# Eight of the token-pair loads of a gated linear attention are issued from ScalarE's queue

## The chip, the cores and the metric

The kernel runs on one core of one Trainium2 chip. The metric is the device time of the whole program in microseconds, lower is better; each kernel is timed in several runs and the median is compared. A profile is one further execution, recorded by the hardware profiler; its span runs from the first to the last instruction of the program, and its own device time is a little longer than its span.

A core has five engines that each work through their own list of instructions in order: TensorE (PE; its weight loads are shown as PEld), VectorE (DVE), ScalarE (ACT), GpSimd (POOL) and SyncE (SP). They wait for each other through semaphores. DMAs are issued here by SyncE and by ScalarE, each into a queue of its own, and both queues are carried by the core's 16 DMA engines.

## The reference

A recurrence with a decaying state for 4 batches of 8 heads, 768 tokens and 48 features, and then a mixer on its output:

```python
for t in range(S):
    state = alpha[:, :, t, :, None] * state + np.einsum('bhd,bhe->bhde', k[:, :, t], v[:, :, t])
    y[:, :, t] = np.einsum('bhd,bhde->bhe', q[:, :, t], state)
...
x = y.transpose(0, 2, 1, 3).reshape(B, S, H * D)
u = x + (x.transpose(0, 2, 1) @ U @ V).transpose(0, 2, 1)
out = u + np.maximum(u @ w_ch1, 0.0) @ w_ch2
```

U is 768 x 32, V 32 x 768, w_ch1 384 x 1536 and w_ch2 1536 x 384; inputs and output are float32.

## The kernel before

Tokens are worked in chunks of 128, six to a batch. A chunk of a batch needs four loads of 192 KB: its alpha, k, q and v, each into one of 40 buffers called `io`. Where a load is done depends on the batch: for all six chunks of batch 0 and the first four of batch 1 two chunks share a stretch of 256 tokens, and a load takes two neighbouring tokens of four heads per partition, in runs of 96 floats (`pload`, L322). These 40 are the token-pair loads. The other chunks take one token of eight heads per partition (`load`, L329). Weights come by L295 and U and V by L270 to L272.

For a chunk, ScalarE takes the logarithm of alpha (`lt`, L352 for a pair, L523 otherwise), TensorE sums it over time (L361 to L368, or L530 and L532), and ScalarE takes exponentials of the sums, `ai` and `aa` and the decay `tot` over the chunk (L375 to L377, or L540, L541 and L543). GpSimd or VectorE multiply k by `ai` and q by `aa` (`rkq`, L383 or L551) and cast v (`rv`, L263 or L267). TensorE transposes the two products (L400 or L564), which are copied from PSUM (`kqt`, L263 or L265), and multiplies them into scores (L424 or L592), which VectorE masks (`pm`, L435 or L602). The state `st` (L473 or L626) passes from chunk to chunk, and the output of the chunk is formed on TensorE (L497 and L507, or L654 and L659). When a batch's chunks are done comes the mixer: a low-rank product (L674, L688), the sum `ub` (L689), transposes, and two large products with the weights (L737 with its relu in L747 or L749, then L763 with the sum in L769 and the store in L774).

The order of all that is written out. The kernel first adds some 1,050 operations to a list, each with a function that takes the name of an engine, and then walks a table of three-character entries: two characters are the number of an operation, the third is the engine that it goes to (P, A, D, G or S for SyncE). Each engine's instructions stand in the order in which the table names them. For a load, the third character says whose queue issues it:

```python
lambda e: (nc.scalar if e == "ACT" else nc.sync).dma_start(
```

A second table gives the buffers; it is the same for both kernels. The semaphores are set by the framework. For DMAs there are eight, DMAHW0 to DMAHW7: each DMA reports its landing on one of them, and it is issued only when the DMA before it on the same semaphore has landed. Which DMA gets which of the eight is dealt out by the framework in the order of the program. An engine that has already waited for a landing does not wait for it again. PSUM has eight banks, which the table of buffers deals to the operations; an operation that takes over a bank waits for the last reader of what was in it.

Of the kernel before, what the change touches and what calls it, by code (L numbers as in the profile page):

```python
# [13 lines left out]

CODE = "ABCDEFGHIJKLMNOPQRSTUVWXYZabcdefghijklmnopqrstuvwxyz0123456789+-"
TABLE = """
BISA8ABASA-AQgAA9SDjAA+SDlPBQSCcACePBKSCzABCSBBSC1PCdACfAABSChACgADnABDSCjDC4AC3ABJSCiDETABES++EClPDqGCkPBMSCnDEVPBRSC6G
CmDDsPBLSEYAC2ACrPDuABSSC5GCoPCsDDmABOSC8PEWACpDAFGC7PC0ABHSCtPCvPCqDC+ADCPDpGDKAC9DBFSCuDEXAC-PDDDBYSCwPEZGDADDEPDrPBUS
DMPDBDDtADkGDGPBGSDNACxDEaGDHPDFDDPADOADvPCyDBTSD8AEbPDIDDyPDJDDLGEcPDoADwDDZPD+PEeAEdDAGPEAABNSDzPDxDAHAEfPBPSD0DDQGEhD
BWSEDGGTABVSDaPAJPGqADbDAASDSPDRGD1PD-AGVPDUDEBAAKADcPD2DGsPGXADdDEUGDTPEgDGWABXSD3PECGEiPD4PEFPGuADVDEjPGtAD5PEHDD9GGvA  # L20
DWPGYABZSD7AGaGD6AEEPEkDElPBgSDYDELPEmPEGADePEMPBaSDXDGZGDfPEIPBcSENDDgPEJDADGEnPBbSDhAEPPGcPEpAEKDGbPDiAAQSEOPGUAEQPEoD
AMSGdAGeDGiPGwGERDEqPAOSESAGjDGfPHaAErPGkDGmPGyPGgDEsAGxGAUSHcPGhDASSE1PE7PHfAG0AE5PAWSE2DGnPHBAEzPE6DBdSGrGGpAGzPGoAEvP
E8DAeSG1AEtPHDPE0DAaSARAANGE9PEuDHGABeSE3PAPGE+AEwDG5PBkSG2PE4DHFAAVGAiSG6DExPHeAFXPHEAATGEyDFZPAXGG7DG9PFYDAgSFBPGlGG4D
FfPAfGFCAE-PHHDFgAAYSFJPG3DHdABiSFAAFdPBoSFaAFFPHIGFeDFKAAcSFhPFGAFHPHzABhSFDPFiAAhGBmSAjAH1PAZGFEDFbPBfSG8GH3AHJPH4AHKP
# [804 lines left out]
```

## Time and profile before

| | |
|---|---|
| median of 3 runs | 159.76 us (158.51 to 160.31) |
| profiled execution | 158.96 us, span 157.2 us, granted clock 1.00 |
| PE | 147.3 us busy, 94% of the span |
| DVE | 107.0 us, 68% |
| ACT | 87.2 us, 55% |
| POOL | 64.6 us, 41% |
| SyncE's DMA queue (q1) | 85808 packets, 28.62 MB |
| ScalarE's DMA queue (q10) | 13536 packets, 2.75 MB |

TensorE counts as busy from the start of a matmul to its modelled end, so a busy share of 94% is not 94% of its peak. A row of the chain of waits gives start, length and what; a row of the timeline gives start, length, engine, line, operation, output and inputs, and in brackets the idle time before it and what ended it. "SPq" and "ACTq" are the sequencers of SyncE and ScalarE that issue DMAs. A row of DMA issues gives the number of DMAs, the size of one, and the median time from issue to landing.

### The profile page before, as it was taken

What the parts mean: (1) busy time and instruction counts of PE and PEld (TensorE: products, weight loads), DVE (VectorE), ACT (ScalarE), POOL (GpSimd) and SP (SyncE); (2) the same over time, 40 slices, a digit from 0 to 9 for tenths busy, and PEclk for the clock granted to TensorE, in tenths of its full rate; (3) what the DMA queues carried; (4) which work ended last, traced back from release to release, by engine and by line L of the source; (5) the groups of instructions that cost most, each with busy time, mean ns of one, the idle gap of its engine ahead of it and who ended that gap; (6) DMA issues with size and microseconds to landing.
All of it is one profiled execution on the core that took longest, in us unless ns stands there. A gap on an engine that the chain in (4) does not pass through costs nothing.

```text
span 157.2 us, 4460 instructions
## 1 busy us (share of the span) xinstructions
PE 147.3 (94%) x1708; PEld 97.5 (62%) x1708; DVE 107.0 (68%) x235; ACT 87.2 (55%) x226; POOL 64.6 (41%) x103
## 2 busy tenths in 40 slices
PE   0898998899999999999999999999999999999991
PEld 0567785566666656667667766666667565566561
DVE  6159998883878658986985948775798463435152
ACT  3858877869797636659788473358713102460000
POOL 8069865656868050275289246155412000000000
PEclk9999999999999999999999999999999999999999
DMA  5999889999999999899999899599780056875234
GB/s 124 323 327 320 230 198 253 277 311 278 251 264 293 246 266 219 151 200 238 206 238 169 139 231 135 116 209 217 145 198 23 0 104 160 263 222 135 74 126 174
DMA packets 99364, 31.64 MB, mean 201 GB/s; under 512 B 93040, under 2 KB 99312, under 8 KB 99344
## 3 DMA queue, kind: packets, MB, share of 16 engines
q1 hardware_dynamic: 85808, 28.62, 77.9%
q10 hardware_dynamic: 13536, 2.75, 9.1%
q8 instruction: 13, 0.21, 0.6%
q14 instruction: 7, 0.06, 0.1%
HBM read 23.89 MB, written 4.72 MB: 182 GB/s over the span
## 4 chain that ended last, share of the span: by engine, by line
PE 77%; SPq 14%; DMA 3%; ACT 1%; issue 1%; POOL 1%; DVE 1%; ACTq 0%
PE ps L763 30%; PE ps L737 29%; SPq L322 12%; DMA io<-in_alpha_dram 3%; PE ps L592 2%; PE ps L564 2%; PE ps L688 2%; PE ps L659 2%; PE ps L530 1%; PE ps L654 1%; PE ps L615 1%; PE ps L708 1%; SPq L270 1%; PE ps L674 1%; PE ps L400 1%
## 5 line engine op out<-in xcount | busy, mean ns | idle before, releaser
L763 PE MATMUL ps<-w_sb,h1t 128*128 128x384 bf16 (+2 forms) x300 | 53.2, 320 | 0.0
L737 PE MATMUL ps<-uT,w_sb 128*128 128x384 bf16 x288 | 51.2, 326 | 0.0
L747 ACT ACTIVATE h1t<-ps 128x384 bf16<-128x384 f32 x57 | 25.9, 501 | 20.9 <-PE ps L737 20.9
L763 PEld LDWEIGHTS <-h1t 128*128 128x128 bf16 x300 | 27.2, 97 | 16.1 <-issue 1.0
L737 PEld LDWEIGHTS <-w_sb 128*128 128x128 bf16 x288 | 27.0, 98 | 16.0
L749 DVE TENSOR_SCALAR h1t<-ps 128x384 bf16<-128x384 f32 x39 | 20.8, 554 | 12.5 <-PE ps L737 12.2
L769 DVE TENSOR_TENSOR io<-ub,ps 128x384 f32<-128x384 bf16 (+2 forms) x25 | 13.2, 536 | 11.3 <-PE ps L763 10.6
L602 DVE TENSOR_TENSOR pm<-ps,maskc 128x512 bf16<-128x512 f32 x28 | 17.7, 683 | 1.0 <-PE ps L592 0.8
L551 POOL TENSOR_TENSOR rkq<-io,ai 128x384 bf16<-128x384 f32 x11 | 10.2, 935 | 14.2 <-DMA io<-in_k_dram 6.6
L689 DVE TENSOR_TENSOR ub<-xb,ps 128x384 bf16<-128x384 bf16 x24 | 12.1, 551 | 2.8 <-PE ps L688 2.7
L551 POOL TENSOR_TENSOR rkq<-io,aa 128x384 bf16<-128x384 f32 x12 | 10.9, 912 | 7.1 <-PE ps L763 3.5
L435 DVE TENSOR_TENSOR pm<-ps,maskp 128x512 bf16<-128x512 f32 x20 | 13.1, 684 | 0.3
L263 ACT CAST xb<-ps 128x192 bf16<-128x192 f32 (+1 forms) x24 | 9.1, 402 | 5.9 <-DVE io L769 2.5
L383 POOL TENSOR_TENSOR rkq<-io,aa 128x384 bf16<-128x384 f32 x9 | 8.2, 918 | 9.2 <-ACT aa L376 4.1
L263 ACT COPY kqt<-ps 128x512 bf16<-128x512 bf16 x18 | 10.5, 595 | 1.5 <-PE ps L400 0.7
L626 POOL TENSOR_TENSOR st<-sm,tot 128x384 bf16<-128x384 f32 x6 | 5.0, 828 | 12.7 <-DVE sm L642 10.7
L267 POOL CAST w_sb<-io 128x384 bf16<-128x384 f32 x16 | 8.1, 514 | 4.6 <-DMA io<-in_moe_w_ch_dram 4.4
L541 ACT ACTIVATE aa<-ps 128x384 bf16<-128x384 f32 x14 | 6.9, 504 | 5.1 <-PE ps L532 4.4
L543 ACT ACTIVATE tot<-ps,off 128x4 f32<-128x4 f32 x22 | 5.9, 278 | 6.4 <-PE ps L532 6.4
L267 POOL CAST rv<-io 128x384 bf16<-128x384 f32 x17 | 8.8, 526 | 1.2 <-DMA io<-in_v_dram 1.1
L265 DVE COPY kqt<-ps 128x512 bf16<-128x512 bf16 x18 | 7.4, 418 | 2.9 <-PE ps L564 1.3
L400 PE MATMUL ps<-ident,rkq 128*128 128x128 bf16 x80 | 8.0, 232 | 1.3 <-ACT lt L352 0.6
(109 smaller groups left out, 214.8 us busy)
## 6 DMA issues: line engine op xcount, KB each, us to landing
io<-in_k_dram SPq DMA_DIRECT2D x24, 192.0 KB, 4.1
io<-in_q_dram SPq DMA_DIRECT2D x24, 192.0 KB, 4.4
io<-in_moe_w_ch_dram SPq DMA_DIRECT2D x24, 192.0 KB, 3.9
io<-in_alpha_dram SPq DMA_DIRECT2D x23, 192.0 KB, 4.2
io<-in_v_dram ACTq DMA_DIRECT2D x13, 192.0 KB, 4.2
out_dram<-io SPq DMA_DIRECT2D x13, 192.0 KB, 2.0
io<-in_v_dram SPq DMA_DIRECT2D x11, 192.0 KB, 3.8
out_dram<-io SPq DMA_DIRECT2D x20, 96.0 KB, 2.2
```

The lines of the kernel that those rows point to most:

```text
L263: nc.scalar.copy(dst, src)
L267: nc.gpsimd.tensor_copy(dst, src)
L322: lambda e: (nc.scalar if e == "ACT" else nc.sync).dma_start(t().rearrange("p (h j) d -> p h (j d)", j=2), src[b, hs, sl, :].rearrange("h ...
L435: nc.vector.tensor_tensor(dst, s2, maskp.to_broadcast([C, 2, 2, C]), op=ALU.mult)
L551: eng.tensor_tensor(dst()[:, :, 0:D], a(), x(), op=ALU.mult)
L602: nc.vector.tensor_tensor(pm()[:, :, par, :], s2, maskc.to_broadcast([C, HP, C]), op=ALU.mult)
L689: P.add(f"u {b}.{c}", lambda e, c=c, hb=hb: nc.vector.tensor_tensor(ub()[:, c, :], xb()[:, c, :], hb()[:, 0:DM], op=ALU.add), r=[hb] + xk( ...
L737: nc.tensor.matmul(hb()[:, 0:TW], lhsT=w1_sb[:, ct, jt * 128 : (jt + 1) * 128], rhs=u_half(uT, ct, tt, b in QUEUE_U), start=(ct == 0), sto ...
L747: nc.scalar.activation(dst, hb()[:, 0:TW], AF.Relu)
L749: nc.vector.tensor_scalar_max(dst, hb()[:, 0:TW], 0.0)
L763: nc.tensor.matmul(hb()[:, 0 : hi - lo], lhsT=h1()[:, jt, c * C : (c + 1) * C], rhs=w2_sb[:, jt, lo:hi], start=(jt == 0), stop=(jt == NJ - 1),
L769: P.add(f"out_{hi - lo} {b}.{c}", lambda e, hb=hb, lo=lo, hi=hi: nc.vector.tensor_tensor(flat(ou)[:, lo:hi], ub()[:, c, lo:hi], hb()[:, 0 ...
```

## The change

Of the 40 token-pair loads in the order of the table, numbers 13, 16, 19, 22, 25, 28, 31 and 34 (every third; the twelfth to the thirty-third when counted from zero) get an A in place of the S. They stay at the same place in the table. Four belong to batch 0 (alpha and v of chunk 2, v of chunk 3, k of chunk 4) and four to batch 1 (alpha and k of chunk 0, v of chunk 1, alpha of chunk 3). The first lines of the diff that differ, in pieces:

```diff
-...ABJSCiDETABES++EClPDq...
+...ABJSCiDETABEA++EClPDq...
-CmDDsPBLSEYAC2A...
+CmDDsPBLAEYAC2A...
```

No other entry differs: TensorE, VectorE and GpSimd have the same instructions in the same order, ScalarE has 8 DMAs more and SyncE 8 fewer. But every DMA's semaphore is dealt anew, so waits differ on all engines.

On ScalarE, near the start (`lt` of the first chunks), the order before (-) and now (+), with the semaphores that an instruction waits for in brackets:

```order
 L376 ACTIVATE aa2_180<-ps_212 128x384
 L352 ACTIVATE lt0_76<-io6_139 128x8x48 [waits DMAHW6_49,Activation_49]
+L322 DMA io12_145<-in_alpha_dram 128x4x96 [waits DMAHW4_49]
+L322 DMA io15_148<-in_v_dram 128x4x96
 L377 ACTIVATE tot2_186<-ps_212 128x8 [waits PE_49]
 L375 ACTIVATE ai1_182<-ps_212 128x384
```

Two loads now stand between the logarithm of io6_139 and the L377 behind it. Further on in ScalarE's order:

```order
 L263 CAST rv1_174<-io10_143 128x384 [waits DMAHW3_49]
+L322 DMA io18_151<-in_v_dram 128x4x96 [waits DMAHW2_49]
 L263 COPY kqt2_190<-ps_212 128x512 [waits PE_49]
-L352 ACTIVATE lt1_77<-io12_145 128x8x48 [waits DMAHW5_49]
+L352 ACTIVATE lt1_77<-io12_145 128x8x48 [waits DMAHW4_49]
 L376 ACTIVATE aa0_178<-ps_212 128x384 [waits Activation_49]
+L322 DMA io21_154<-in_alpha_dram 128x4x96 [waits DMAHW5_49]
 L263 COPY kqt1_189<-ps_212 128x512 [waits PE_49]
```

The load into io21_154, which SyncE issued, now stands behind an exponential (L376), and reports on DMAHW5 (it waits for the DMA before it there). On SyncE the order of the same place was, from the load into io15_148 on:

```order
L322 DMA io15_148<-in_v_dram 128x4x96 [waits DMAHW0_49]
L322 DMA io16_149<-in_q_dram 128x4x96 [waits DMAHW1_49]
L322 DMA io17_150<-in_q_dram 128x4x96 [waits DMAHW2_49]
L322 DMA io18_151<-in_v_dram 128x4x96 [waits DMAHW3_49]
L322 DMA io19_152<-in_k_dram 128x4x96 [waits DMAHW4_49]
L322 DMA io20_153<-in_alpha_dram 128x4x96 [waits DMAHW5_49]
L322 DMA io21_154<-in_alpha_dram 128x4x96 [waits DMAHW6_49]
```

and is now:

```order
L322 DMA io16_149<-in_q_dram 128x4x96 [waits DMAHW1_49]
L322 DMA io17_150<-in_q_dram 128x4x96 [waits DMAHW3_49]
L322 DMA io19_152<-in_k_dram 128x4x96 [waits DMAHW4_49]
L322 DMA io20_153<-in_alpha_dram 128x4x96 [waits DMAHW6_49]
L322 DMA io22_155<-in_q_dram 128x4x96 [waits DMAHW7_49]
L322 DMA io23_156<-in_v_dram 128x4x96 [waits DMAHW0_49]
L322 DMA io25_158<-in_v_dram 128x4x96 [waits DMAHW1_49]
L322 DMA io26_159<-in_q_dram 128x4x96 [waits DMAHW3_49]
L270 DMA ue_in_69<-in_moe_U_dram 64x6x32 [waits DMAHW5_49]
```

The three loads into io15_148, io18_151 and io21_154 are gone from it, and those that stay wait for other semaphores: io19_152 for DMAHW4, on which ScalarE's io12_145 reports, io20_153 for DMAHW6 (ScalarE's io15_148), and ue_in for DMAHW5 (ScalarE's io21_154).

On ScalarE near 80 us of the profile of before, where batch 2 is worked beside the mixer of batch 1, the order is the same but for the waits. Before:

```order
L540 ACTIVATE ai2_183<-ps_212 128x384
L329 DMA io26_159<-in_v_dram 128x8x48 [waits DMAHW2_49]
L543 ACTIVATE tot0_184<-ps_212,off_129 128x4 [waits Pool_49]
L263 CAST rv0_173<-io18_151 128x384 [waits DMAHW6_49]
L540 ACTIVATE ai1_182<-ps_212 128x384 [waits Activation_49]
L543 ACTIVATE tot1_185<-ps_212,off_129 128x4
L541 ACTIVATE aa2_180<-ps_212 128x384
```

and now:

```order
L540 ACTIVATE ai2_183<-ps_212 128x384
L329 DMA io26_159<-in_v_dram 128x8x48 [waits DMAHW4_49]
L543 ACTIVATE tot0_184<-ps_212,off_129 128x4 [waits Pool_49]
L263 CAST rv0_173<-io18_151 128x384 [waits DMAHW1_49]
L540 ACTIVATE ai1_182<-ps_212 128x384 [waits Activation_49]
L543 ACTIVATE tot1_185<-ps_212,off_129 128x4
L541 ACTIVATE aa2_180<-ps_212 128x384
```

The v load into io26_159 waited for DMAHW2 and waits for DMAHW4 now. Which DMA reports on DMAHW4 there is to be seen on GpSimd, in the instructions that read what was loaded:

```order
 L626 TENSOR_TENSOR st3_200<-sm1_196,tot2_186 128x384 [waits DVE_49]
-L551 TENSOR_TENSOR rkq2_81<-io20_153,ai1_182 128x8x48 [waits DMAHW5_49,PE_49]
-L267 CAST rv1_174<-io24_157 128x384 [waits DMAHW7_49]
-L551 TENSOR_TENSOR rkq2_81<-io25_158,aa0_178 128x8x48 [waits DMAHW0_49,Activation_49]
+L551 TENSOR_TENSOR rkq2_81<-io20_153,ai1_182 128x8x48 [waits DMAHW4_49,PE_49]
+L267 CAST rv1_174<-io24_157 128x384 [waits DMAHW2_49]
+L551 TENSOR_TENSOR rkq2_81<-io25_158,aa0_178 128x8x48 [waits DMAHW6_49,Activation_49]
```

The k load into io20_153 reported on DMAHW5 and reports on DMAHW4 now; it is the last DMA on DMAHW4 ahead of the one into io26_159.

More of the change, by code (lines that the diff above doesn't have):

```diff
@@ L16 @@
 TABLE = """
[L17 to L21, printed above, removed]
+BISA8ABASA-AQgAA9SDjAA+SDlPBQSCcACePBKSCzABCSBBSC1PCdACfAABSChACgADnABDSCjDC4AC3ABJSCiDETABEA++EClPDqGCkPBMSCnDEVPBRSC6G
+CmDDsPBLAEYAC2ACrPDuABSSC5GCoPCsDDmABOSC8PEWACpDAFGC7PC0ABHACtPCvPCqDC+ADCPDpGDKAC9DBFSCuDEXAC-PDDDBYSCwPEZGDADDEPDrPBUA
+DMPDBDDtADkGDGPBGSDNACxDEaGDHPDFDDPADOADvPCyDBTSD8AEbPDIDDyPDJDDLGEcPDoADwDDZPD+PEeAEdDAGPEAABNADzPDxDAHAEfPBPSD0DDQGEhD
+BWSEDGGTABVADaPAJPGqADbDAASDSPDRGD1PD-AGVPDUDEBAAKADcPD2DGsPGXADdDEUGDTPEgDGWABXSD3PECGEiPD4PEFPGuADVDEjPGtAD5PEHDD9GGvA
+DWPGYABZSD7AGaGD6AEEPEkDElPBgADYDELPEmPEGADePEMPBaSDXDGZGDfPEIPBcSENDDgPEJDADGEnPBbADhAEPPGcPEpAEKDGbPDiAAQSEOPGUAEQPEoD
 AMSGdAGeDGiPGwGERDEqPAOSESAGjDGfPHaAErPGkDGmPGyPGgDEsAGxGAUSHcPGhDASSE1PE7PHfAG0AE5PAWSE2DGnPHBAEzPE6DBdSGrGGpAGzPGoAEvP
```

## The prediction

> **What bounds the kernel now.** I read the page first, then the chain of waits in order of time, then the busy time by stretches, then single DMAs.
>
> ```profile
> span 157.2 us, 4460 instructions
> PE 77%; SPq 14%; DMA 3%; ACT 1%; issue 1%; POOL 1%; DVE 1%; ACTq 0%
> 0.73 0.46 SPq L322
> ...
> 22.87 0.51 SPq L322
> 23.42 5.30 DMA io<-in_alpha_dram
> 28.80 0.53 ACT lt L352
> 29.34 0.40 PE ps L400 x4
> ```
>
> The second line is the page's summary of the chain that ended last: TensorE holds 77% of the span and SyncE's queue 14%. The rows below are that chain in time (start, length, what). Up to 23.42 us it is one token-pair load after another on SyncE (L322), a new one every 0.55 us; then it waits 5.30 us for one alpha load to land, and from 29.34 it lies on TensorE. So the front, up to 29 us, waits for loads, and everything behind it is TensorE's. Read like that, the issuing of loads is the front's bound. The next view says otherwise.
>
> ```profile
> 4.50:10.00 5.50, 5.45 (x39) 3.60 (x39) 1.83 (x4) 3.52 (x11) 1.84 (x2) 1.00 1.17 325
> 10.00:15.00 5.00, 4.40 (x103) 3.48 (x102) 3.91 (x10) 4.15 (x11) 3.99 (x6) 1.00 1.17 319
> 15.00:20.00 5.00, 5.00 (x111) 3.91 (x111) 4.98 (x15) 4.47 (x14) 4.29 (x6) 1.00 0.95 248
> 20.00:25.00 5.00, 4.58 (x129) 3.55 (x128) 4.78 (x11) 3.79 (x14) 3.69 (x7) 1.00 0.86 198
> 25.00:29.40 4.40, 3.53 (x82) 2.16 (x82) 3.81 (x10) 2.91 (x8) 1.68 (x2) 1.00 0.97 283
> ...
> 90.00:130.00 40.00, 40.00 (x392) 25.19 (x389) 28.54 (x55) 17.34 (x46) 12.34 (x17) 1.00 0.73 138
> ```
>
> The first figure behind the stretch's length is TensorE's busy time; the last three are the granted clock, the share of the 16 DMA engines and GB/s. From 4.5 to 15 us the DMA engines move 319 to 325 GB/s at a share of 1.17: a load of 192 KB takes 0.61 us there, longer than the 0.55 us between two issues. The engines that carry the packets are the bound, not the queue that asks for them. From 15 to 29.4 us they move less. The last row shows TensorE busy for 40.00 of 40.00 us: a delay that reaches it before 90 us is not made good behind.
>
> **The change, part by part.** *Eight issues leave SyncE.* Seven of them stand ahead of the alpha load at 23.42. By issue time alone that is 7 x 0.55 = 3.9 us. But bytes set the pace. At 322 GB/s throughout, the three slow stretches would be shorter by 5.0 x (322-248)/322 = 1.2, 5.0 x (322-198)/322 = 1.9 and 4.4 x (322-283)/322 = 0.5 us, 3.6 us in all: that is the largest gain a second issuer can bring. Whether two queues move more than one is shown in the trace: in 3.4 to 6.4 us both carry loads, in 6.4 to 9.4 us SyncE's alone.
>
> ```profile
> DMA packets 2608, 0.97 MB, mean 323 GB/s; under 512 B 2608, under 2 KB 2608, under 8 KB 2608
> q1 hardware_dynamic: 1876, 0.70, 84.6%
> q10 hardware_dynamic: 732, 0.27, 32.7%
> ...
> DMA packets 2438, 0.99 MB, mean 329 GB/s; under 512 B 2406, under 2 KB 2406, under 8 KB 2438
> q1 hardware_dynamic: 2438, 0.99, 116.6%
> ```
>
> 323 GB/s with two queues (q1 SyncE's, q10 ScalarE's), 329 with one: nothing is gained by a second queue as such. The Trainium skill's page "DMA: Bandwidth & Descriptors", section "Issuing engines are not separate DMA queues", says that DMAs run on the same 16 engines whoever starts them, and that issuing from several engines only saves the sequencers' time to start them. The trace agrees on the first half (323 against 329 GB/s); taken by its second half alone the front would be 3.9 us shorter, which is a rival below.
>
> *SyncE may not run ahead.* In the change its load into io20_153 waits for DMAHW6, which ScalarE's io15_148 holds; ue_in waits for DMAHW5, which ScalarE's io21_154 holds. In the trace of before these two, then SyncE's, were issued and landed so:
>
> ```profile
> 9.46 0.52 SPq L322 DMA_DIRECT2D io<-in_v_dram  x1
> io<-in_v_dram SPq DMA_DIRECT2D x1, 192.0 KB, 3.8
> 12.53 1.12 SPq L322 DMA_DIRECT2D io<-in_alpha_dram  x2
> io<-in_alpha_dram SPq DMA_DIRECT2D x1, 192.0 KB, 5.1
> ```
>
> The v load into io15_148 (9.46, 3.8 us to landing) landed at 13.3, but io20_153 was issued at 12.53, the first of the two in that row. With the new wait it goes out 0.7 us late, however early SyncE gets there. The second of that row, io21_154, took 5.1 us to land, 1.3 more than 3.8: that much work is in line ahead of it and covers the 0.7. So the lead that SyncE wins it spends waiting. For the front I take +0.3 us, between 0 (the line covers it) and 0.7 (it does not). The far ends are -3.6 (all the missing bytes won back) and 8 x 0.51 = +4.1 (all eight issues on ScalarE's path at the 0.51 us of the row of 22.87).
>
> *Eight issues come to ScalarE.* One of ScalarE's own issues took 0.61 us at the start of the program; a late one takes 0.37 (the row of 79.57, in the next fence). At the place of the first two new ones it had idle time:
>
> ```profile
> 1.23 0.61 ACTq L322 DMA_DIRECT2D io<-in_v_dram  x1
> 10.38 0.18 ACT L377 ACTIVATE tot<-ps 128x8 f32<-128x8 f32 x1 [1.93 <-PE ps L368]
> ```
>
> The first two new ones stand ahead of the L377 that had 1.93 us of idle time before it, which hides 2 x 0.51 us. The others I also cost at nothing. ScalarE's sequencer starts a DMA while earlier instructions are still in line for its engine (next fence: 79.57, ahead of the L540 of 80.17 that comes before it in the program), and the work behind follows without a gap. If that cover is gone, it is 0.5 us each.
>
> *The semaphores are dealt anew.* Each DMA reports on one of eight, and may start only when the earlier DMA on it has landed. With eight loads on another engine the deal differs far down the program. In one place this adds a wait that ends late: ScalarE's v load into io26_159 waited for DMAHW2 and now waits for DMAHW4, on which the k load into io20_153 reports.
>
> ```profile
> 75.47 0.85 SPq L329 DMA_DIRECT2D io<-in_k_dram  x1
> io<-in_k_dram SPq DMA_DIRECT2D x1, 192.0 KB, 6.0
> 79.57 0.37 ACTq L329 DMA_DIRECT2D io<-in_v_dram  x1
> 80.17 0.50 ACT L540 ACTIVATE ai<-ps 128x384 bf16<-128x384 f32 x1
> 80.54 0.29 ACT L543 ACTIVATE tot<-ps,off 128x4 f32<-128x4 f32 x1
> 81.62 0.54 ACT L541 ACTIVATE aa<-ps 128x384 bf16<-128x384 f32 x1
> 81.99 0.32 ACT L543 ACTIVATE tot<-ps,off 128x4 f32<-128x4 f32 x1
> 82.91 0.57 ACT L541 ACTIVATE aa<-ps 128x384 bf16<-128x384 f32 x1
> 83.54 1.07 ACT L263 COPY kqt<-ps 128x512 bf16<-128x512 bf16 x2
> 83.96 0.33 PE L654 MATMUL ps<-st,kqt 128*128 128x96 bf16 x4
> ```
>
> That k load landed 6.0 us after 75.47, at 81.47. ScalarE asked at 79.57, so its sequencer stands still for 1.90 us; with 0.37 us for the issue it is free at 81.84. Queued behind are L543 (it began at 80.54) and the exponentials, casts and copies to the copies of kqt. The engine still has the work up to 80.54, so the delay is 81.84 - 80.54 = 1.30 us. Who waits: TensorE's L654, at 83.96, takes over the PSUM bank that the aa of 82.91 reads, and that ended at 83.48, 0.48 us before; it comes 1.30 - 0.48 = 0.8 us late. The copies of kqt began 0.63 us behind that aa, where 0.37 is enough (81.62 to 81.99), so they take up 0.26 of the delay and are 1.0 us late; the next matmuls wait for them too. Between 0.8 and 1.0 I take 0.9 us on TensorE, and the row of 90 to 130 us has no idle time to give back. From both sides:
>
> ```profile
> io<-in_k_dram SPq DMA_DIRECT2D x24, 192.0 KB, 4.1
> io<-in_q_dram SPq DMA_DIRECT2D x1, 192.0 KB, 6.9
> ```
>
> With the median of 4.1 us the k load would land at 79.57 and nothing would be lost; with the 6.9 us of a q load that follows it it would be 0.9 us more, 1.8 in all. I take 0.9, since both DMAs and the instructions around them are the same as in this execution.
>
> **The sum**, against the profiled execution's 158.96 us (157.2 of span and 1.8 around it): 158.96 + 0.3 (front) + 0 (issues on ScalarE) + 0.9 (wait at 79.57) = 160.16 us. The median of the runs, 159.76, is 0.80 above the profiled one, so the forecast is 161.0 us, 0.8% over the median. The measurement tells about 1% from no change.
>
> **Rivals.** *Faster: the front is set by issuing.* If the slow stretches from 15 us on come from one queue that stands still, ScalarE's queue fills them, at most by the 3.6 us above: 155.4, against the median 156.2 us. It decides if the DMA engines run at about 322 GB/s to the end of the front. For it speak the chain of waits, which is SyncE's issues up to 23.42, and the 198 GB/s from 20 to 25 us. Against it speak the full rate up to 15 us, and that SyncE has to wait for ScalarE's landings. It would have to outweigh the 0.9 us as well. Chance 0.16, a part of the gain included.
>
> *No difference.* The k load lands before ScalarE asks, as with the median of 4.1 us, and the front comes out even: 158.96, or 159.8 us. For it speaks that the landing has ranged from 4.1 to 6.9 us in these rows; against it, that many loads are in line at 75 us, whichever run it is. Chance 0.19.
>
> *Slower still: loads behind waiting instructions.* ScalarE's k load into io24_157 stands behind L376 at 16.95; SyncE had issued it at 15.47:
>
> ```profile
> 15.47 1.38 SPq L322 DMA_DIRECT2D io<-in_k_dram  x1
> 16.95 0.49 ACT L376 ACTIVATE aa<-ps 128x384 bf16<-128x384 f32 x1
> 20.11 0.91 POOL L383 TENSOR_TENSOR rkq<-io,ai 128x384 bf16<-128x384 f32 x1
> io<-in_k_dram SPq DMA_DIRECT2D x1, 192.0 KB, 4.5
> ```
>
> It landed 4.5 us after 15.47, at 19.97, and GpSimd read it at 20.11, with 0.14 us to spare. Issued 1.5 us later, it delays GpSimd and with it the front by up to 1.5: 158.96 + 1.5 + 0.9 = 161.36, against the median 162.2 us, and other waits on landings could add to it. Against it: the sequencer runs ahead of its engine, and TensorE may catch up before 90 us. Chance 0.23.
>
> **How the numbers follow.** The forecast has 0.42. It lies so near to 1% over the median (161.36) that I split it into 0.20 slower, 0.21 within and 0.01 faster. The slower rival adds 0.23; the rival of no difference gives 0.16 within and 0.03 slower; the faster one 0.16. Together: faster 0.17, same 0.37, slower 0.46. The range of 158.2 to 163.2 us leaves out most of the faster rival, and at the top what lies more than 1.0 us beyond the slower rival, 0.9 of it being what the wait at 79.57 may be longer.
>
> **What would show it.** In the changed profile q10 carries eight loads more. Right: SyncE issues no earlier than now around 12.5 us, the rate up to 15 us stays at about 320 GB/s, and ScalarE's L543 near 80.5 us is preceded by over 1 us of idle time, with TensorE's L654 late by nearly as much. Wrong: the alpha load at the end of the front lands over 2 us earlier than 28.7 and TensorE keeps that lead to 90 us; or that k load lands before ScalarE asks; or ScalarE shows gaps at each of the eight issues.

## The result and the profile after

The change makes the kernel faster: 158.28 us in the median of 20 runs (157.15 to 162.71) against 159.56 us of before in 20 runs (158.41 to 162.22). The ratio is 0.9932, with a 95% interval of 0.9908 to 0.9956. The forecast was 161.0 us, slower by 0.8%. The program runs in two states, and every ratio here compares executions in the faster one alone, while the medians are of all, so a ratio need not be that of its medians.

The profiled execution took 158.35 us with a span of 156.5 us. The page of the changed kernel, its span and the summary of the chain of waits:

```profile
span 156.5 us, 4458 instructions
PE 75%; DMA 11%; ACT 7%; issue 1%; POOL 1%; DVE 1%; ACTq 1%; SPq 0%; POOLq 0%; DVEq 0%
```

SyncE's queue, 14% of the chain before, is all but gone from it (0%), and waits for single landings (DMA, 11%) stand in its place. The same chain in time (start, length, what), at the places that follow:

```profile
16.71 3.72 DMA io<-in_k_dram
20.59 0.92 POOL rkq L383
29.34 0.81 ACT uT L263
43.60 4.09 DMA io<-in_k_dram
47.85 0.92 POOL rkq L551
65.21 2.93 PE ps L737 x18
74.20 5.75 DMA io<-in_k_dram
86.00 0.78 PE ps L592 x24
142.66 10.68 PE ps L763 x76
```

The same places in the chain of the kernel before:

```profile
30.88 0.81 ACT uT L263
66.07 2.93 PE ps L737 x18
86.50 0.78 PE ps L592 x24
143.32 10.68 PE ps L763 x76
```

The copy to uT ends the front in both, and it comes 1.54 us earlier. At the matmuls of 65.21 the lead is 0.86 us, at 86.00 it is 0.50, and at the last group 0.66, which is the difference of the spans (0.7). So the front gained 1.54 us, 0.68 was lost again by 65 us (GpSimd waits up to 47.7 us for the k load issued at 43.60), 0.36 by 86 us (the k load issued at 74.20), and 0.16 came back behind.

Busy time by stretches, changed kernel (columns as before: TensorE first, at the end clock, DMA share and GB/s):

```profile
4.50:10.00 5.50, 5.44 (x47) 3.70 (x47) 1.82 (x4) 3.53 (x11) 1.85 (x2) 1.00 1.17 320
10.00:15.00 5.00, 4.18 (x114) 3.31 (x115) 4.27 (x11) 4.51 (x13) 4.13 (x6) 1.00 1.17 324
15.00:20.00 5.00, 4.82 (x94) 3.54 (x95) 4.97 (x14) 4.42 (x14) 4.11 (x6) 1.00 1.13 298
20.00:25.00 5.00, 4.92 (x154) 4.01 (x151) 4.69 (x12) 3.90 (x15) 4.51 (x8) 1.00 1.09 267
25.00:29.40 4.40, 4.40 (x83) 3.10 (x82) 4.30 (x11) 3.78 (x13) 2.66 (x5) 1.00 0.96 307
44.00:50.00 6.00, 5.20 (x78) 3.20 (x77) 4.21 (x10) 4.38 (x11) 4.83 (x9) 1.00 0.98 274
```

Up to 15 us the rate stayed: 320 and 324 GB/s against 325 and 319. Behind it the rate rose from 248, 198 and 283 to 298, 267 and 307 GB/s. How it looked inside one slow stretch, from 19.5 to 24 us in 40 slices (busy share of the DMA engines in tenths, and GB/s), before:

```profile
DMA  9999999999999999995222020166447999999999
GB/s 246 239 273 280 280 277 290 446 300 301 290 256 239 245 213 194 185 150 84 30 31 28 13 93 20 38 99 96 56 112 205 290 314 314 307 301 321 324 324 311
```

and after:

```profile
DMA  9999999999999999999999999997779998999997
GB/s 328 321 328 324 328 299 268 253 240 202 233 400 269 305 307 290 262 260 294 302 312 290 299 260 311 304 253 205 167 237 244 198 218 225 218 222 222 218 212 215
```

For 1.2 us (19th to 29th slice of 0.11 us each, 13 to 99 GB/s) the 16 DMA engines of the kernel before stood nearly idle, although five to seven loads were issued and had not landed. In the changed kernel the gap is not there.

The alpha load that ended the wait of the front before (issued at 23.42, landed at 28.72) is issued at 21.26 now and lands at 25.68, 3.04 us earlier:

```profile
21.26 0.97 SPq L322 DMA_DIRECT2D io<-in_alpha_dram  x1
```
```profile
io<-in_alpha_dram SPq DMA_DIRECT2D x1, 192.0 KB, 4.4
```

Only half of that reaches the copy to uT, since the chain now waits for the k load issued at 16.71 instead.

### The profile page after: what moved, and what is told of

It is laid out like the page before. It is cut to its first block, busy times and chain, and to the rows that moved or that the text cites. A ratio compares the mean times of both kernels' runs of the same rounds, so it can differ in the third digit from the quotient of the medians.

```text
span 156.5 us, 4458 instructions
## 1 busy us (share of the span) xinstructions
PE 146.7 (94%) x1708; PEld 97.2 (62%) x1708; DVE 107.3 (69%) x235; ACT 86.9 (56%) x226; POOL 65.0 (42%) x103
## 4 chain that ended last, share of the span: by engine, by line
PE 75%; DMA 11%; ACT 7%; issue 1%; POOL 1%; DVE 1%; ACTq 1%; SPq 0%; POOLq 0%; DVEq 0%
PE ps L763 28%; PE ps L737 25%; DMA io<-in_k_dram 9%; PE ps L688 3%; PE ps L400 2%; DMA io<-in_alpha_dram 2%; PE ps L592 2%; PE ps L659 2%; ACT kqt L263 1%; PE ps L424 1%; PE ps L507 1%; PE ps L654 1%; PE ps L674 1%; PE ps L708 1%; PE ps L530 1%
## 5 line engine op out<-in xcount | busy, mean ns | idle before, releaser
L383 POOL TENSOR_TENSOR rkq<-io,aa 128x384 bf16<-128x384 f32 x9 | 8.2, 920 | 6.5 <-ACT aa L376 4.1
L267 POOL CAST rv<-io 128x384 bf16<-128x384 f32 x17 | 9.3, 557 | 1.1 <-DMA io<-in_v_dram 1.1
L543 ACT ACTIVATE tot<-ps,off 128x4 f32<-128x4 f32 x22 | 5.8, 273 | 7.0 <-PE ps L532 6.4
```

The lines of the kernel that those rows point to most:

```text
L267: nc.gpsimd.tensor_copy(dst, src)
```

## The experiments

How many loads were in flight is counted from the trace, each from the start of its issue to its landing. The table gives the mean number from 16.5 to 26 us beside the rate in the same stretch and the start of the uT copy ("clock fell" where the granted clock dropped ahead of that copy, so that it can't be compared); the ratio is to the kernel before, timed on the same chip.

| kernel | median us (n) | ratio, 95% interval | in flight, all (SyncE's) | GB/s | uT copy at us |
|---|---|---|---|---|---|
| before | 159.56 (20) | | 5.6 (5.6) | 208 | 30.88 |
| changed, the first time | 158.28 (20) | 0.9932, 0.9908 to 0.9956 | 7.2 (5.5) | 287 | 29.34 |
| changed, again (f1) | 158.27 (12) | 0.9947, 0.9916 to 0.9979 | 7.2 (5.4) | 265 | 29.92 |
| first four only (e2) | 158.77 (12) | 0.9975, 0.9939 to 1.0012 | 5.4 (5.4) | 223 | 30.67 |
| last four only (e3) | 161.52 (12) | 1.0093, 1.0047 to 1.0139 | 5.5 (4.0) | 211 | 32.06, clock fell |
| last four, idle matmuls (g1) | 159.73 (10) | 1.0030, 0.9997 to 1.0063 | 5.2 (3.6) | 198 | 31.63 |
| k load back to SyncE (e4) | 157.88 (12) | 0.9921, 0.9883 to 0.9958 | 6.4 (5.2) | 262 | 31.91, clock fell |
| v load later (e1) | 157.64 (12) | 0.9913, 0.9875 to 0.9951 | 7.3 (5.6) | 261 | 29.58 |
| k load earlier (f2) | 158.22 (13) | 0.9950, 0.9921 to 0.9980 | 6.7 (5.4) | 245 | 32.42, clock fell |
| k earlier, v later (f3) | 157.88 (9) | 0.9916, 0.9888 to 0.9945 | 7.2 (5.5) | 282 | 29.09 |
| the same, idle matmuls (g2) | 158.57 (12) | 0.9954, 0.9928 to 0.9979 | 7.1 (5.5) | 267 | 30.24 |
| one queue, fewer pieces (f4) | 158.82 (8) | 0.9972, 0.9928 to 1.0016 | 6.4 (6.4) | 256 | 30.82, clock fell |
| the same, idle matmuls (g3) | 158.19 (5) | 0.9945, 0.9907 to 0.9984 | 7.0 (7.0) | 273 | 30.26 |
| 13 loads on ScalarE (h1) | 164.48 (6) | 1.0363, 1.0312 to 1.0414 | 7.5 (5.7) | 301 | 35.16, clock fell |

With 5.2 to 5.6 loads in flight go 198 to 223 GB/s, with 6.4 to 7.5 go 245 to 301. Within the second group the two do not go together (7.3 at 261, 6.4 at 262), and the number in flight is also a result of the rate and of the time to landing. So the table alone does not say which of them drives the other; the experiments are to show it.

### Which of the eight bring the gain (e2 and e3)

The first four alone, the other four back on SyncE (the entries in which the kernel differs from the changed one):

```diff
-BNA
-BVA
-BgA
-BbA
+BNS
+BVS
+BgS
+BbS
```

> Only the first four of the eight loads on ScalarE (into io12_145, io15_148, io18_151, io21_154); the other four on SyncE as before. Theory A (the gain is that two queues together hold more loads in flight while one DMA engine is behind, which fills the stretches at 17, 22 and 25 us in which the DMA engines of the kernel before stood nearly idle): these four have landed by 16.3 us, so at most the stretch at 17 us is filled, 20 to 25 us stays near 200 GB/s, the uT copy near 30.9 us comes at most 0.4 us earlier, and the time is within 0.5 us of the kernel before. Theory B (the gain is issue time taken off SyncE, evenly per load): half of the 1.5 us at the front, the uT copy near 30.1 us, and a time 0.5 us or more under the kernel before.

The copy to uT came 0.21 us earlier than before, and the time can't be told from that of before. Theory B, a gain per load taken off SyncE, wanted 0.75 us and is out. Theory A had expected this. Where the time went that SyncE saved is to be seen on its queue:

```profile
15.06 2.39 SPq L322 DMA_DIRECT2D io<-in_v_dram  x1
```

The issue of one load took 2.39 us there, where many others take 0.51; the changed kernel has the same at 14.99 (2.38 us), the kernel before has shorter ones (1.15 and 1.38 us at 14.28 and 15.47). So what SyncE saves it spends standing at a later issue.

The last four alone:

```diff
-BEA
-BLA
-BHA
-BUA
+BES
+BLS
+BHS
+BUS
```

> Only the last four of the eight loads on ScalarE (into io24_157, io27_160, io30_163, io33_166); the other four on SyncE as before. Theory A (more loads in flight while one DMA engine is behind): these four are in flight between 16.7 and 26.3 us, so 20 to 25 us moves over 250 GB/s, 7 or 8 loads are in flight in place of 5 or 6, and most of the 1.5 us at the front is there: uT copy at 29.7 us or earlier. Theory B (issue time, evenly per load): half of it, the uT copy near 30.1 us.

Both were wrong: slower than before by 0.9%, and no more loads in flight. SyncE's waits between 12 and 28 us say why (line, waited for, us in total, times, longest):

```profile
SPq L270 <- DMA io<-in_k_dram: 2.4, 1, 2.4
SPq L295 <- DMA io<-in_alpha_dram: 1.6, 1, 1.6
```

```profile
16.19 0.37 ACTq L322 DMA_DIRECT2D io<-in_k_dram  x1
20.01 1.63 SPq L270 DMA_DIRECT2D ue_in<-in_moe_U_dram  x2
```

ScalarE issued the k load into io24_157 at 16.19 us, behind a copy that waits for TensorE. ue_in, a few DMAs further on in SyncE's order, reports on the same semaphore, so SyncE stood until that load landed, at 20.0 us, with only 4.0 of its own loads in flight in the mean. In the changed kernel ue_in waits for ScalarE's io21_154 instead, which had been issued at 11.56 us. So this is the prediction's "SyncE may not run ahead", at a higher price than was said.

A second thing happened in that execution. TensorE waited 1.11 us for GpSimd (the bracket is the idle time before), and behind it the granted clock fell; the last figure but two in each row is the clock:

```profile
18.14 0.45 PE L458 MATMUL ps<-rv,rkq 64*128 64x96 bf16 x8 [1.11 <-POOL rkq L383]
```

```profile
17.00:18.00 1.00, 0.03 (x4) 0.00 (x0) 0.78 (x2) 0.08 (x1) 0.89 (x2) 1.00 1.08 285
18.00:19.00 1.00, 0.86 (x10) 0.39 (x11) 0.36 (x1) 0.83 (x2) 1.00 (x3) 0.62 0.93 246
19.00:20.00 1.00, 1.00 (x9) 0.81 (x9) 0.40 (x2) 0.99 (x4) 1.00 (x2) 0.50 1.16 318
20.00:21.00 1.00, 1.00 (x12) 0.80 (x10) 0.60 (x4) 0.44 (x2) 1.00 (x2) 0.50 0.84 230
21.00:22.00 1.00, 1.00 (x18) 0.99 (x17) 0.79 (x3) 0.94 (x4) 1.00 (x3) 0.67 0.41 67
```

At 0.62, 0.50, 0.50 and 0.67 of the clock TensorE lost 1.7 us of work in 4 us. In all 12 runs of this kernel the mean clock was 0.989 or less; 0.989 is what this execution had.

### Clock or SyncE's wait (g1)

The kernel of e3 with five matmuls on zeros ahead of the L458 that waits:

```diff
         def f_d(e):
+            if (b, u) == (0, 2):
+                for _ in range(5):
+                    nc.tensor.matmul(db[1](), lhsT=filler[:, 0:128], rhs=filler, start=True, stop=True)
             for n in range(4):
```

> The kernel with only the last four loads on ScalarE, and five idle matmuls on zeros (128x512 each, results overwritten) on TensorE just ahead of the L458 that waits 1.11 us for GpSimd at 18.14 us, after which the granted clock there fell to 0.50 for some 3 us. Theory C (the lower clock after TensorE's pause makes the last four slow): the clock stays at 1.00 between 18 and 22 us, the uT copy comes at 30.9 us or earlier instead of 32.06 us, the median falls by 1.2 us or more from 161.5 us. Theory L (SyncE's wait of 2.4 us for the landing of ScalarE's k load decides, through the alpha load that it issues at 23.45 us): the clock stays at 1.00, the uT copy remains near 32 us and the median over 160.5 us.

The clock stayed at 1.00 from 15 to 25 us in the profile, and the ratio fell from 1.0093 to 1.0030: some 0.6%, 1 us, of what the last four lost was the clock, though the two intervals overlap, so the size is rough. The rest stayed: the uT copy at 31.63 us, SyncE's longest wait 3.3 us. Both theories hold a part. Even at full clock the last four alone bring nothing (what the idle matmuls cost is in that).

### How many loads one queue holds (f4 and g3)

Is it the second queue, or the number of loads in flight? The kernel before, all loads on the queues of before, with 11 of SyncE's loads as one contiguous piece (the lines behind it have numbers higher by 9):

```diff
+                if (b, c, src.tensor.name.split("_")[1]) in WIDE:
+                    P.add(
+                        f"pload {b}.{c}",
+                        lambda e: nc.sync.dma_start(flat(t), src[b].rearrange("h s d -> (h s d)")[0 : 128 * DM].rearrange("(p f) -> p f", p=128)),
+                        w=[t],
+                    )
+                    return
```

> The kernel before, every load on its queue as before, but 11 of SyncE's loads issued from 14 to 24 us (v of b0 c5, k and v of b0 c4, q, k, v of b1 c0, alpha of b1 c3, k, q, v of b1 c1, alpha of b1 c2) fetch the same 192 KB as one contiguous piece, 1536 bytes per partition in place of four runs of 384, from other places of the same tensor: so the values computed from them are not the reference's, the work behind is the same. Theory A (one queue holds only 5 or 6 of these loads at a time because of their many pieces, and the DMA engines run dry when one of them is behind): 7 or 8 loads are in flight from 17 us on, no stretch between 16.5 and 26 us falls under 250 GB/s, the uT copy comes 1.5 us or more earlier than the 30.88 us of the kernel before, without a second queue. Part of that is that longer pieces move faster (a weight load of that form landed every 0.5 us, against 0.6 us for a token-pair load: 11 x 0.1 = 1.1 us). Theory B (SyncE's issue time of 0.55 us each, or something that comes at fixed times, holds the loads up): still 5 or 6 in flight, the stretches at 17, 22 and 25 us still under 200 GB/s, uT copy at 30.3 us or later.

In the mean 6.8 loads were in flight from 16.5 to 20.5 us, 5.7 from 21.5 to 24. In this execution TensorE paused for 1.08 us at 17 us and the clock fell, so its uT copy, 30.82 us, says little. With the five idle matmuls:

> The kernel before with the 11 contiguous loads (192 KB each, 1536 bytes per partition, values not the reference's), and the five idle matmuls at the same place, so that the clock stays at 1.00. Theory A (one queue holds too few of the many-pieced loads): 7 or 8 in flight, the uT copy at 29.9 us or earlier, against 30.88 us in the kernel before. Theory B (issue time, or something at fixed times): uT copy at 30.5 us or later in spite of the full clock.

Seven in flight in the mean (7.1 and 7.3 in the same two stretches), at full clock, and a ratio of 0.9945: the size of the change's gain, from one queue. The uT copy, 30.26 us, lies between what the two theories wanted (29.9 or earlier, 30.5 or later); the idle matmuls may cost part of that (g2). The stretch from 16.5 to 26 us in one row each, before, first four, changed, and fewer pieces with idle matmuls:

```profile
16.50:26.00 9.50, 9.07 (x234) 6.93 (x232) 8.95 (x22) 7.65 (x23) 7.25 (x10) 1.00 0.87 208
```
```profile
16.50:26.00 9.50, 8.96 (x231) 6.83 (x228) 8.79 (x22) 7.42 (x23) 6.99 (x10) 1.00 0.91 223
```
```profile
16.50:26.00 9.50, 9.24 (x237) 6.96 (x235) 9.06 (x23) 7.89 (x25) 7.97 (x11) 1.00 1.11 287
```
```profile
16.50:26.00 9.50, 9.47 (x223) 7.11 (x221) 8.40 (x21) 7.52 (x23) 7.97 (x11) 1.00 0.94 273
```

5.6, 5.4, 7.2 and 7.0 loads in flight go with 208, 223, 287 and 273 GB/s. Part of the last is that longer pieces move faster, estimated at 1.1 us for the 11 loads in the expectation, so this run shows the number in flight more firmly than it shows the time. A third thing differs: SyncE's issue of a load in long pieces takes 0.43 us and not 0.51, which makes 0.9 us for 11 loads, and it stands less at single issues (1.07 and 1.16 us at most, for 1.38 and 1.49). A quicker issue and more loads in flight are not separated here; against the quicker issue alone speaks the first-four kernel, where 2 us of saved issue time brought 0.21 us.

### More on the second queue (h1)

13 loads, every second one from the thirteenth to the thirty-seventh of the order:

```diff
-BES
-BRS
-BSS
...
-BdS
-BkS
+BEA
+BRA
+BSA
...
+BdA
+BkA
```

> 13 token-pair loads on ScalarE in place of 8: every second one from the thirteenth to the thirty-seventh of the order (alpha, v, q, k of b0 c2 and others), the places in the order unchanged. If more on the second queue is better (SyncE's issue time), the uT copy comes before 29.3 us and the time is under the changed kernel's, a ratio to the kernel before of 0.990 or less. Theory A with its limit (in flight are at most 8, one for each semaphore, and the changed kernel already has 7 or 8; every further load on ScalarE is issued behind an instruction that waits, and SyncE then waits for its landing): still at most 8 in flight, SyncE's waits for landings between 10 and 30 us add up to more than the 4 us of the changed kernel, no further gain: uT copy at 29.3 us or later, a ratio of 0.995 or more.

The second theory was right in its sign and far too mild: 3.6% slower, SyncE's waits for landings 7.0 us in all (10 to 30 us; 2.5 us in the profile of the changed kernel). No other kernel here moved more in this stretch, 301 GB/s. The chain shows what for:

```profile
22.49 5.27 DMA io<-in_v_dram
27.79 5.41 DMA io<-in_alpha_dram
```

```profile
20.18 5.14 SPq L295 DMA_DIRECT2D io<-in_moe_w_ch_dram  x8
```

SyncE, rid of 13 loads, began with the weights at 20.18 us (24.53 before), while ScalarE issued the loads that the front needs behind instructions that waited: the alpha load that was issued at 23.42 us before (into io32_165) only at 27.79. Bytes moved, but the wrong ones first. TensorE's clock fell here too (0.53 in the mean from 20 to 25 us); how much of the 3.6% is the clock and how much the late loads was not split.

### The k load that comes late (e4, f2) and the v load near 80 us (e1, f3)

e4 gives the k load into io24_157 back to SyncE (BNA to BNS). f2 leaves it on ScalarE, two instructions earlier:

```diff
-...D+PEeAEdDAGPEAABNADzP...
+...D+PBNAEeAEdDAGPEAADzP...
```

> Seven loads on ScalarE: the k load into io24_157, which ScalarE issued only at 16.71 us, behind an exponential, is SyncE's again. Theory (its late landing, 20.43 us, is what holds up GpSimd's L383 at 20.59 us and with it the front): it is issued before 15.5 us and lands by 19.9 us, L383 begins 0.3 to 0.5 us earlier than 20.59 us, and the uT copy comes at 28.9 to 29.1 us instead of 29.34 us; the end gains up to 0.3 us of that. Rival (ScalarE's and TensorE's own work sets the front by now, or the load takes a place in SyncE's queue that others need): uT copy at 29.3 us or later, the time as the changed kernel's.

> The changed kernel with ScalarE's k load into io24_157 two instructions earlier in ScalarE's order, ahead of the copy to kqt that waits for TensorE (L263 near 16.2 us); it stays ScalarE's, and the order of the loads among each other stays the same. Theory (the load is late because ScalarE's sequencer stands at that copy; the front then waits for it at L383): issued near 15.7 us in place of 16.71 us, landed by 20.0 us in place of 20.43 us, L383 near 20.2 us in place of 20.59 us, uT copy 0.3 to 0.4 us earlier than in the changed kernel, time 0.2 to 0.4 us less. Rival (the front is now set by the DMA engines' bytes or by the engines' own work): the load is early and nothing behind it moves; time the same.

e1 moves the v load into io26_159 behind the third exponential (its letter in the table of buffers moves with it); f3 has the moves of e1 and f2:

```diff
-...K4PCHAJjPNbAJODK+ALEGNZAK5D...
+...K4PJjPNbAJODK+ALEGNZACHAK5D...
```

> The changed kernel with ScalarE's v load into io26_159 (near 80 us) three instructions further on in ScalarE's order, behind the exponential that works on ai1; all else, the semaphores too, as in the changed kernel. Theory (the wait for the landing of the k load into io20_153, which holds up ScalarE there, costs the end 0.36 us): L543 behind it begins near 79.7 us instead of 80.39 us, L654 near 83.1 us instead of 83.35 us, and the span is about 0.4 us shorter than the changed kernel's 156.5 us, so 156.1 us. Rival (TensorE makes it good by 90 us, or another wait ends last in its place): L543 early all the same, span 156.5 us.

> The changed kernel with both moves: the k load into io24_157 two instructions earlier on ScalarE, and ScalarE's v load into io26_159 (near 80 us) three instructions later. Theory: the two gains add up, 0.3 + 0.36 us less than the changed kernel, a ratio to the kernel before of about 0.989. Rival for the second: its wait is made good elsewhere, and the time is that of the first move alone.

> The changed kernel itself, beside the two that follow on the same chip. Expected: a ratio to the kernel before of 0.993 as in the first comparison; in the profile 7 or 8 loads in flight from 18 to 24 us, over 250 GB/s there, L383 of the k load into io24_157 near 20.5 us, and ScalarE's L543 near 80.4 us preceded by idle time.

In times, none of the four can be told from the changed kernel: 0.9913 to 0.9950 against 0.9932 and 0.9947, with intervals that overlap. The lowest ratios, 0.9913 (e1) and 0.9916 (f3), beat the kernel before, but not the changed one beyond doubt. Of what was expected of f1, the loads in flight came (7.2 in the mean from 18 to 24 us); the rate stayed under 250 GB/s there (244), L383 began at 21.18 us and not near 20.5, and nothing waited ahead of L543. The profiles tell more. For the k load, GpSimd's L383 that reads it, in f1 and then in f3:

```profile
21.18 0.91 POOL L383 TENSOR_TENSOR rkq<-io,ai 128x384 bf16<-128x384 f32 x1 [1.16 <-DMA io<-in_k_dram]
```
```profile
20.04 0.92 POOL L383 TENSOR_TENSOR rkq<-io,ai 128x384 bf16<-128x384 f32 x1
```

With the load earlier the wait of 1.16 us is gone and the uT copy comes at 29.09 in place of 29.92 us. That is one execution each, and the wait differs between executions: with the load at the place of f1, L383 began at 20.59 in the first profile and at 20.44 in e1, with the uT copy at 29.34 and 29.58. So the move is worth between 0.25 and 0.83 us at the uT copy by these. (In the profiled executions of e4 and f2 TensorE pauses near 17 us and the clock falls, so their fronts can't be compared; L383 began at 20.27 in e4, as expected, and at 20.55 in f2, not at 20.2.) For the v load, f1 shows that the wait is not always there:

```profile
78.32 0.44 ACTq L329 DMA_DIRECT2D io<-in_v_dram  x1
82.70 0.33 PE L654 MATMUL ps<-st,kqt 128*128 128x96 bf16 x4
```
```profile
io<-in_k_dram SPq DMA_DIRECT2D x1, 192.0 KB, 3.9
```

In this execution of the same program the k load took 3.9 us, landed before ScalarE asked, and L654 comes 1.26 us earlier than before, the whole lead that TensorE had at 66 us (64.81 against 66.07). In the profiled executions of e1 and f3 the k load landed before ScalarE asked as well (3.7 and 3.8 us from issue to landing, at 76.2 and 75.6 us), so there the move had no wait to remove. Only the first profile of the changed kernel has this wait, and what e1 removes over many runs stays open.

A lead at 83 us is not yet one at the end. In f1 TensorE kept 1.25 us to 97 us and finished only 0.6 us earlier than before, because it stood for 0.50 us between 90 and 130 us, where neither the kernel before nor the first profile has a pause. Nearly all of that is a wait for a transposing DMA that landed at 113.65:

```profile
90.00:130.00 40.00, 39.50 (x376) 24.65 (x373) 28.21 (x53) 16.33 (x42) 11.04 (x16) 1.00 0.73 133
```
```profile
109.32 4.33 DMA kqt<-rkq
```

The profiled executions of e1 and f3, with spans of 155.4 and 155.3 us, kept their leads nearly whole (1.59 and 2.08 us at 97 us).

### Idle matmuls in the better version (g2)

> The changed kernel with both moves (k load two instructions earlier, v load near 80 us three later) and the five idle matmuls at the same place. Theory: executions in which TensorE pauses there and the clock falls (3 of 20 of the changed kernel, 4 of 9 of the one with both moves) disappear, so the median falls to about 157.4 us and the spread narrows; where there is no pause the 1 us of matmuls is made good by 29 us, since the front waits for loads. Rival: they cost TensorE up to 1.05 us in every execution, median 158.5 us or more.

By the median the rival was right, although the kernel before took longer on this chip too (159.28 us, for 158.83 beside f3). The spread narrowed (157.47 to 159.27 us) and the clock was 0.997 or more in all 12 runs, but the ratio, 0.9954, is 0.4% above f3's 0.9916 (0.6 us). That ratio does not count the four of f3's nine executions whose clock fell (0.975 to 0.989; 160.13 to 161.18 us), and g2 has none of these. So it shows what the idle matmuls cost where the clock stays up; whether they save more than that over all executions is not shown.

## Why the prediction was wrong

**The front, +0.3 us, is the step that failed.** It gave -1.54 us in the profile (-0.96 to -1.79 in f1, e1 and f3). Its far end, -3.6 us, was computed from the right rows, the missing bytes behind 15 us, and some 40% of it came. (The first term of that sum is 1.15 and not 1.2 us; the 3.6 holds.) The mistake was the choice between the far ends. I tested whether a second queue moves more in the stretch from 3.4 to 9.4 us, where 323 against 329 GB/s said no. But there nothing stood still: with 6.3 loads in flight (4.5 to 15 us), nearly all of them SyncE's, the rate was full. The missing bytes lay where the one queue held 5.6 loads and the engines ran dry at 13 to 99 GB/s; a view of that stretch would have said that the engines were not the bound there. The prediction's own row of 15.47, an issue of 1.38 us where others take 0.51 to 0.54, was a sign that the queue that asks stood still too. The rival in which the slow stretches come from one queue that stands still, and ScalarE's queue fills them, described it and got 0.16. That 158.28 us lies just inside the stated range of 158.2 to 163.2 us is luck: the sign was wrong.

The Trainium skill's page "DMA: Bandwidth & Descriptors", section "Issuing engines are not separate DMA queues", says that several issuing engines save only the sequencers' time. Issue time alone does not give these runs: the first four, at 0.51 us saved each, brought 0.21 us in all, and the gain went with the loads in flight (5.6 to 7.2, 208 to 287 GB/s), also without a second queue (7.0, 273 GB/s, with the shorter issues said above).

**SyncE may not run ahead: right that it waits, wrong that this takes the gain away.** In the changed kernel SyncE waits for landings, which no row of before has (10 to 30 us):

```profile
SPq L322 <- DMA io<-in_v_dram: 1.2, 2, 0.9
SPq L322 <- DMA io<-in_alpha_dram: 0.8, 1, 0.8
```

```profile
12.79 0.37 SPq L322 DMA_DIRECT2D io<-in_alpha_dram  x1
```

The load into io20_153 went out at 12.79 us, 0.26 later than before (0.7 was said). While SyncE waited, ScalarE's loads were under way. Where ScalarE's load itself is late, as in e3, SyncE's wait (2.4 us) is longer than the whole gain.

**Eight issues at nothing: right for all but one.** ScalarE shows no gap of 0.5 us at them. The one is the rival "loads behind waiting instructions": the k load into io24_157 went out at 16.71 us, 1.24 late, and L383 began at 20.59 in place of 20.11. Its place was right, its price 0.48 us and not 1.5, because the load needed 3.72 us and not 4.5.

**The wait near 80 us, +0.9 us, came with the right mechanism and the wrong size:** 0.36 us in the profiled execution, and nothing in f1, e1 and f3.

```profile
79.97 0.38 ACTq L329 DMA_DIRECT2D io<-in_v_dram  x1
80.39 0.26 ACT L543 ACTIVATE tot<-ps,off 128x4 f32<-128x4 f32 x1 [0.57 <-POOL rkq L551]
83.35 0.33 PE L654 MATMUL ps<-st,kqt 128*128 128x96 bf16 x4
```

Against its place before less the lead of 0.86 us (79.68) L543 is 0.71 us late, not 1.30, and L654 (83.10) 0.25. The way from one to the other was as worked out: 0.71 less the 0.48 of room is 0.23. What failed is the reason given, that both DMAs "are the same as in this execution": SyncE issued the k load 1.27 us earlier than before (74.20 for 75.47) while ScalarE came 0.86 earlier, and the landing took 5.75 us here and 3.9 in f1.

**"TensorE keeps that lead to 90 us"** was named, with the alpha load over 2 us earlier, as what would show the forecast wrong. The alpha load came 3.04 us earlier; of TensorE's lead of 1.54 us at 29 us a third was left at 90 (0.50 us), and in f1 all of it (1.25). What I had not seen is that between 44 and 50 us a later lead is limited by the k load of 43.60 us (TensorE 5.20 us busy of 6.00). In f1 TensorE is busy all 6.00 us there, so this too differs from execution to execution.

## What to carry to other kernels

Before a front is called bound by bytes, read the rate stretch by stretch and count the loads in flight: where the DMA engines fell idle with five to seven loads issued, more loads in flight filled the gap here, by a second queue and, less firmly shown, by loads of fewer pieces. The second queue helped only as long as its loads were issued in time: one that stands behind a waiting instruction holds up, through the shared semaphores, the queue it was meant to relieve (e3), and 13 in place of 8 turned a gain of 0.7% into a loss of 3.6%. A wait for a landing is one that some executions have and others not: the same k load took 3.7 to 6.0 us in five profiles. Price it as a chance, not as a term.

## What the runs showed of the hardware

From 16.5 to 26 us SyncE's queue held 5.4 to 5.6 of the 192 KB loads in 384-byte pieces in the mean, whatever ScalarE's did (before, changed, e2), and 7.0 when 11 of them were in 1536-byte pieces. That is no fixed limit: from 4.5 to 15 us the kernel before held 6.2. Why the DMA engines stand still at 17, 22 and 25 us was not tried. In each of these stretches of the kernel before one packet of another queue falls, the instruction queue's (13.5 to 18.5 us, its packets, MB and time as a share of 16 engines):

```profile
q8 instruction: 1, 0.02, 1.3%
```

That is 1.0 us if one engine carries it (0.013 x 16 x 5 us, an estimate). The changed kernel has the same packet in the first two of these stretches without the engines standing still there, so the packet alone is not the cause; whether it has a part is not shown.

A pause of TensorE of 1.1 us near 17 us (1.11 in e3, 1.08 in f4) was followed by 3.4 us at half the granted clock (the 1.7 us of work lost in e3 are 3.4 us at 0.50). Two pauses within 4 us were so followed in e4 (0.72 and 0.62 us) and, for 6.8 us, in f2 (0.67 and 0.99), but not in e1 (0.71 and 0.91); nor were single ones of 1.04 us in g1 (at 25.7 us) and e4 (at 27.8), and of 0.61 us in f1. So the length of a pause alone does not decide. The Trainium skill's page "TensorE: Matmul & The Clock Gate", section "Part 1: The HAM clock gate (the "warmup" mystery)", gives an idle window of about 3.4 us for the fall; in e3 and f4 a third of that was enough. What decides whether the pause comes is not shown.
